# Attention and max-out FFN on one core: the second batch's softmax weights split undivided, its weighted sums divided, and an epsilon moved from VectorE to ScalarE

## The chip, the cores and the metric

The kernel runs on one core of a Trainium2 chip. The metric is the device time of one execution in microseconds (us); a comparison takes the median of several executions. A profile is one further execution, recorded with the start and the length of each instruction on TensorE (PE, its weight loads as PEld), VectorE (DVE), ScalarE (ACT), GpSimd (POOL) and the DMA queue that SyncE (SP) feeds.

## The reference

```python
# q, k, v: (8 batches, 12 heads, 448 rows, 64), float32
q_n, k_n = rmsnorm(q, g_q), rmsnorm(k, g_k)
scores = q_n @ k_n.T / sqrt(64)
attn = exp(scores - max(scores))              # "undivided" weights
attn = attn / (sum(attn) + 1e-9)              # "divided" weights
x = (attn @ v), heads side by side            # 3584 tokens x 768
h = maximum(maximum(x @ w1, x @ w2), x @ w3)  # three 768 x 768 layers
out = h @ w_out
```

## The kernel before

**Groups and quarters.** A group `g` is one batch's pair of heads, and there are 48: batch 0 is groups 0 to 5, the second batch 6 to 11, and so on. Each group is worked in four quarters `c` of 112 query rows. The quarter's scores for both heads (2 x 448 columns) lie in a PSUM tile `sc`, of which there are two in turn. So the scores of quarter c+2 can't start before the last reader of quarter c's tile is done.

**The first batch** (`g < PLAIN = 6`) multiplies in float32. Its exponentials go to SBUF and are turned by TensorE; the sums of a row's exponentials go to a tile `sum`. One group later the sums get their epsilon (`guard_sums`, ScalarE, L619), are inverted (`inverse_sums`, VectorE, L623), are spread over the 64 columns of a head by eight small float32 matmuls (`spread_sums`, L631), are copied to SBUF (`keep_sums`, ScalarE, L641), and multiply the weighted sums in PSUM (`scale_plain`, VectorE, L711).

**All later groups** split each operand into a float16 and a float16 rest, and add three products. A quarter runs like this:

- `scores` (L553, PE): six matmuls into `sc`.
- `row_max` (L562, DVE): the negated maximum of both heads' rows.
- `softmax` (L570 and L579, ACT): the scaled maximum `nm`, then one exponential for each head, written back into `sc`; the row sums go beside them in PSUM, each by a record named ACTIVATION_READ_ACCUMULATOR.
- `upper_weights`: the divisor `rs`, made by two VectorE instructions (L648: epsilon and scaling, L652: reciprocal); then ScalarE writes the divided float16 weights, one instruction for each head (L655).
- `lower_weights` (L665, DVE): the float16 rests, one instruction for each head. This one frees `sc`.
- `turn_weights`: a DMA transpose of both parts into `pt`. A group later `add_values` (L703, PE) multiplies with the values, and `finish` (L717 on ACT, L718 on DVE) splits the weighted sums into `xt`.

**The order** is written out by hand: `beat(g, i)` issues, for each of a group's twelve beats, attention work, and `thirds` fills in matmuls of the FFN of an earlier batch (L732 for the three layers, L796 for the last; their PSUM tiles `acc`, three buffers under the tag `m`, are read by `hidden`: L742 ACT, L746 DVE, L752 ACT, L756 DVE). Of a quarter, beat 3c issues the exponentials, beat 3c+1 `upper_weights`; what is due in between, such as the float16 copy of the next keys (`upper_rows`, L434) in each group's first quarter, stands between the two on ScalarE. Each engine works its own list in order. During the first two batches VectorE also decodes the float64 weights (L196, L200, L205 and others). The values of group g+6 are loaded in group g (`load_v`, `vr`, eight buffers), on SyncE's list, where key, query and weight loads and the transposes follow.

## Time and profile before

| what | before |
|---|---|
| time, median of 3 | 1100.64 us (1097.57 to 1104.33) |
| the profiled execution's own time | 1099.43 us |
| its span, first to last instruction | 1097.6 us |
| mean granted TensorE clock | 0.964 |
| PE busy | 1011.4 us (92%) |
| ACT busy | 771.8 us (70%) |
| DVE busy | 755.7 us (69%) |
| POOL busy | 704.2 us (64%) |

A group row of the page has: line, engine, operation, tile written<-tiles read, number of instructions; then the time in which at least one of them ran and the mean length of one in ns; then the idle time of the engine just before them, and what ended most of it. In a timeline row the first two numbers are start and length in us, and a bracket holds the idle time before. A row of waits has the total in us, the number, and the longest. A row of stretches has the length, each engine's busy time (with its instructions), the granted TensorE clock, the DMA share and GB/s.

### The profile page before, as it was taken

What the parts mean: (1) busy time and instruction counts of PE and PEld (TensorE: products, weight loads), DVE (VectorE), ACT (ScalarE), POOL (GpSimd) and SP (SyncE); (2) the same over time, 40 slices, a digit from 0 to 9 for tenths busy, and PEclk for the clock granted to TensorE, in tenths of its full rate; (3) what the DMA queues carried; (4) which work ended last, traced back from release to release, by engine and by line L of the source; (5) the groups of instructions that cost most, each with busy time, mean ns of one, the idle gap of its engine ahead of it and who ended that gap; (6) DMA issues with size and microseconds to landing.
All of it is one profiled execution on the core that took longest, in us unless ns stands there. A gap on an engine that the chain in (4) does not pass through costs nothing. (4 is left out here: it accounts for less than half of the span.)

```text
span 1097.6 us, 18387 instructions
## 1 busy us (share of the span) xinstructions
PE 1011.4 (92%) x6168; PEld 499.4 (45%) x6168; DVE 755.7 (69%) x1390; ACT 771.8 (70%) x1767; POOL 704.2 (64%) x805
## 2 busy tenths in 40 slices
PE   4678769888899999999999999999999999999998
PEld 2333334334444454444544454444444554445554
DVE  4799988888767676777677767777676766761110
ACT  4598888767878687787877787777777787863101
POOL 5477988866767777677777776777777677610000
PEclk9697869999999999999999999999999999999999
DMA  5554566855887779778887798787877797553002
GB/s 152 164 168 149 131 183 135 192 116 121 164 156 143 145 153 179 152 148 144 168 156 147 138 168 172 148 145 155 174 145 140 140 178 142 108 100 73 1 1 57
DMA packets 426493, 152.28 MB, mean 139 GB/s; under 512 B 372896, under 2 KB 422048, under 8 KB 426400
## 3 DMA queue, kind: packets, MB, share of 16 engines
q1 hardware_dynamic: 425888, 150.95, 67.7%
q8 instruction: 48, 0.79, 0.3%
q14 instruction: 45, 0.37, 0.1%
q10 hardware_dynamic: 512, 0.18, 0.1%
HBM read 51.97 MB, written 11.01 MB: 57 GB/s over the span
## 5 line engine op out<-in xcount | busy, mean ns | idle before, releaser
L732 PE MATMUL acc<-xt,w_sb 128*128 128x448 f16 x2592 | 516.8, 355 | 0.0
L732 PEld LDWEIGHTS <-w_sb 128*128 128x128 f16 x2592 | 244.1, 98 | 259.3 <-issue 47.9
L579 ACT ACTIVATE sc<-sc,nm,down 112x448 f32<-112x448 f32 x336 | 234.2, 697 | 11.2
L562 DVE TENSOR_REDUCE sc<-sc 112x2 f32<-112x896 f32 x192 | 209.6, 1092 | 46.0 <-PE sc L553 44.7
L655 ACT ACTIVATE pp<-sc,rs 112x448 f16<-112x448 f32 x336 | 194.8, 632 | 46.6 <-ACT sc L579 40.9
L665 DVE SCALAR_TENSOR_TENSOR pp<-sc,rs,pp 112x448 f16<-112x448 f32 x336 | 212.9, 675 | 3.4 <-ACT pp L655 2.9
L387 POOL TENSOR_TENSOR ri<-ri,half_neg 128x7 f32<-128x7 f32 x96 | 154.2, 1606 | 8.0
L553 PE MATMUL sc<-kt,qt 64*112 64x448 f16 x1008 | 131.9, 367 | 28.8 <-DVE pp L665 25.0
L570 ACT ACTIVATE nm<-sc,down 112x2 f32<-112x2 f32 x192 | 50.7, 264 | 147.5 <-DVE sc L562 146.1
L796 PE MATMUL acc<-wo_sb,ht 128*128 128x384 f16 x864 | 151.0, 329 | 1.5 <-DVE ht L756 0.8
L761 POOL COPY hx<-ht 128x128 f16<-128x128 f16 x48 | 15.5, 323 | 197.1 <-DVE ht L756 191.1
L796 PEld LDWEIGHTS <-ht 128*128 128x128 f16 x864 | 81.6, 99 | 67.2 <-issue 13.5
L703 PE MATMUL av<-pt,vp 128*64 128x448 f16 x1008 | 108.3, 356 | 0.0
L553 PEld LDWEIGHTS <-qt 64*112 64x112 f16 x1008 | 54.8, 126 | 98.3 <-issue 57.8
L648 DVE TENSOR_SCALAR rs<-sc 112x2 f32<-112x2 f32 x168 | 26.6, 158 | 94.6 <-ACT sc L579 94.6
L440 POOL TENSOR_TENSOR kp<-kn,kp 128x512 f16<-128x512 f32 x42 | 50.0, 1191 | 58.9 <-ACT kp L434 58.9
L703 PEld LDWEIGHTS <-vp 128*64 128x64 f16 x1008 | 49.6, 108 | 55.7 <-issue 30.0
L718 DVE SCALAR_TENSOR_TENSOR xt<-av,xt 128x448 f16<-128x448 f32 x42 | 26.2, 625 | 70.8 <-ACT xt L717 70.8
L372 DVE TENSOR_REDUCE ss<-sq 128x7 f32<-128x448 f32 x96 | 60.9, 635 | 10.6 <-ACT sq L363 6.6
L531 POOL TENSOR_TENSOR vp<-vr,vp 128x448 f16<-128x448 f32 x42 | 43.8, 1044 | 30.3 <-ACT vp L525 30.2
L440 POOL TENSOR_TENSOR qp<-qn,qp 112x512 f16<-112x512 f32 x42 | 49.2, 1173 | 19.8 <-ACT qp L434 19.8
L517 POOL TENSOR_SCALAR vr<-vr,v_up 128x448 f32<-128x448 f32 x42 | 61.1, 1456 | 0.0
(112 smaller groups left out, 1200.4 us busy)
## 6 DMA issues: line engine op xcount, KB each, us to landing
raw<-in_moe_w_dram SPq DMA_DIRECT2D x18, 768.0 KB, 4.5
qr<-in_q_dram SPq DMA_DIRECT2D x48, 224.0 KB, 3.1
vr<-in_v_dram SPq DMA_DIRECT2D x96, 96.0 KB, 2.6
kr<-in_k_dram SPq DMA_DIRECT2D x95, 96.0 KB, 3.1
raw<-in_moe_w_out_dram SPq DMA_DIRECT2D x6, 768.0 KB, 5.0
pt<-pp SPq DMA_TRANSPOSE x168, 4.0
out_dram<-osb SPq DMA_DIRECT2D x8, 336.0 KB, 3.2
out_dram<-osb SPq DMA_DIRECT2D x8, 288.0 KB, 3.6
```

The costliest lines, as they stand in the source:

```text
L372: nc.vector.tensor_reduce(sums[g % 2][:sq.shape[0], KQ[what]], sq, axis=AX, op=ALU.add)
L387: nc.gpsimd.tensor_tensor(out=ri, in0=ri, in1=half_neg[:, at], op=ALU.pow)
L440: nc.gpsimd.tensor_tensor(out=parts[:, 1], in0=n, in1=parts[:, 0], op=ALU.subtract)
L517: nc.gpsimd.tensor_scalar(out=vr, in0=vr, scalar1=v_up[:, g // NP:g // NP + 1], scalar2=None, op0=ALU.mult,)
L553: nc.tensor.matmul(sc[:QP, h, :S], qt[rows, qp, c], kt[rows, kp, KEYS[h]], start=n == 0, stop=n == len(TERMS) - 1,)
L562: nc.vector.tensor_reduce(sc[:QP, 0, S + 8:S + 10], sc[:QP, :, :S], axis=AX, op=ALU.max, negate=True)
L579: nc.scalar.activation(to, sc[:QP, h, :S], AF.Exp, bias=nm[:, h:h + 1], scale=down[:QP], accum_out=total,)
L655: nc.scalar.activation(pp[:, 0, h], sc[:QP, h, :S], AF.Copy, scale=rs[:, h:h + 1])
L665: nc.vector.scalar_tensor_tensor(out=pp[:, 1, h], in0=sc[:QP, h, :S], scalar=rs[:, h:h + 1], in1=pp[:, 0, h], op0=ALU.mult, op1=ALU.subtract,)
L703: nc.tensor.matmul(av[half, :S], vp[rows, group, vpart], pt[rows, 7 * wp + group], start=u == 0 and n == 0, stop=u == 3 and n == len(TERMS ...
L732: nc.tensor.matmul(acc[:, :S], wt[:, wp, c], xs[c][:, xp], start=(c == 0 and n == 0), stop=(c == NCT - 1 and n == 2),)
L796: nc.tensor.matmul(acc[:, :HW], lhs, wo_sb[:, f, wp, half * HW:(half + 1) * HW], start=(f == 0 and n == 0), stop=(f == NFT - 1 and n == 2),)
```

## The change

Three things change; a new constant `UNDIVIDED = 12` marks the end of the second batch.

1. Groups 6 to 11 write their weights undivided. The row sums go to `sum`, there is no `rs`, one ScalarE instruction writes `P_UP` times the exponentials of both heads, and one VectorE instruction writes both rests. The weighted sums are divided one group later as in the first batch (`guard_sums` to `scale_plain`). The tile `by` of `keep_sums` gets a buffer of its own in place of one shared with the FFN's `m`, and `vr` has seven buffers in place of eight.
2. Groups 12 to 47 still divide their weights. The epsilon and scaling of `rs` go from VectorE to ScalarE; the reciprocal stays on VectorE.
3. Nothing else in the order of `beat` changes.

```diff
+UNDIVIDED = 12
...
-        load_kv(g, "vr", v, 8)
+        load_kv(g, "vr", v, 7)
...  softmax
+        if g < UNDIVIDED and c == 0:
+            s["sum"] = sb.tile([QP, NQ, 2], F32, name="sum", bufs=2)
         if g < PLAIN:
-            if c == 0:
-                s["sum"] = sb.tile([QP, NQ, 2], F32, name="sum", bufs=2)
             s["e", c] = sb.tile([QP, 2, S], F32, name="e", tag="pp", bufs=3)
         for h in range(2):
             to, total = sc[:QP, h, :S], sc[:QP, 1, S + 8 + h:S + 9 + h]
+            if g < UNDIVIDED:
+                total = s["sum"][:, c, h:h + 1]
             if g < PLAIN:
-                to, total = s["e", c][:, h], s["sum"][:, c, h:h + 1]
+                to = s["e", c][:, h]
...  keep_sums
-        s["by"] = sb.tile([P, S], F32, name="by", tag="m", bufs=2)
+        s["by"] = sb.tile([P, S], F32, name="by", bufs=1)
...  upper_weights
+        if g < UNDIVIDED:
+            pp = s["pp", c] = sb.tile([QP, 2, 2, S], F16, name="pp", bufs=3)
+            nc.scalar.activation(pp[:, 0], sc[:QP, :, :S], AF.Copy, scale=P_UP)
+            return
         rs = sb.tile([QP, 2], F32, name="rs", bufs=3)
-        nc.vector.tensor_scalar(
-            out=rs, in0=sc[:QP, 1, S + 8:S + 10], scalar1=SUM_EPS, scalar2=1.0 / P_UP,
-            op0=ALU.add, op1=ALU.mult,
+        nc.scalar.activation(
+            rs, sc[:QP, 1, S + 8:S + 10], AF.Copy, bias=SUM_EPS / P_UP, scale=1.0 / P_UP
         )
         nc.vector.reciprocal(rs, rs)
...  lower_weights
+        if g < UNDIVIDED:
+            nc.vector.scalar_tensor_tensor(
+                out=pp[:, 1], in0=sc[:QP, :, :S], scalar=P_UP, in1=pp[:, 0],
+                op0=ALU.mult, op1=ALU.subtract,
+            )
+            return
...  beat
-        if 0 <= w < PLAIN:
+        if 0 <= w < UNDIVIDED:
```

VectorE's list in the second batch, from the maximum of group 7's first quarter to the rests of its first quarter. Before (`wo_sb` and `raw` are the decoding of the output weights, `ss` the sums of squares for a later group, `m` and `acc` the FFN):

```order
L562 TENSOR_REDUCE sc<-sc 112x2
L665 SCALAR_TENSOR_TENSOR pp<-sc,rs,pp 112x448 x2
L259 TENSOR_SCALAR w_most<-most 128x1
L262 RECIPROCAL w_up<-w_most 128x1
L263 TENSOR_SCALAR w_up<-w_up 128x1
L200 SCALAR_TENSOR_TENSOR wo_sb<-raw,wo_sb 128x768
L648 TENSOR_SCALAR rs<-sc 112x2
L652 RECIPROCAL rs<-rs 112x2
L205 SCALAR_TENSOR_TENSOR wo_sb<-raw,wo_sb 128x768
L372 TENSOR_REDUCE ss_87<-sq 128x7
```

The same place in the changed kernel, whose lines stand 3 to 15 lower:

```order
L565 TENSOR_REDUCE sc<-sc 112x2
L673 SCALAR_TENSOR_TENSOR pp<-sc,pp 112x896
L262 TENSOR_SCALAR w_most<-most 128x1
L265 RECIPROCAL w_up<-w_most 128x1
L266 TENSOR_SCALAR w_up<-w_up 128x1
L203 SCALAR_TENSOR_TENSOR wo_sb<-raw,wo_sb 128x768
L208 SCALAR_TENSOR_TENSOR wo_sb<-raw,wo_sb 128x768
L628 RECIPROCAL sum<-sum 112x8
L375 TENSOR_REDUCE ss_87<-sq 128x7
```

The two instructions on `rs` are gone, and with them VectorE's need of the exponentials at this place; the reciprocal of the group before's eight sums has come in.

ScalarE's list in the same quarter. Before:

```order
L570 ACTIVATE nm<-sc,down 112x2
L579 ACTIVATE sc<-sc,nm,down 112x448 x2
L434 CAST kp<-kn_90 128x512
L655 ACTIVATE pp<-sc,rs 112x448 x2
L434 CAST qp<-qn 112x512
```

In the changed kernel:

```order
L573 ACTIVATE nm<-sc,down 112x2
L584 ACTIVATE sc,sum<-sc,nm,down 112x448 x2
L437 CAST kp<-kn_90 128x512
L654 ACTIVATE pp<-sc 112x896
L624 ACTIVATE sum<-sum 112x8
L437 CAST qp<-qn 112x512
```

The weights' instruction is one, it no longer reads `rs`, and the epsilon for the group before's sums follows it.

ScalarE's list in a later batch, group 21, first and second quarter. Before:

```order
L570 ACTIVATE nm<-sc,down 112x2
L579 ACTIVATE sc<-sc,nm,down 112x448 x2
L434 CAST kp<-kn_90 128x512
L655 ACTIVATE pp<-sc,rs 112x448 x2
L434 CAST qp<-qn 112x512
L570 ACTIVATE nm<-sc,down 112x2
L579 ACTIVATE sc<-sc,nm,down 112x448 x2
L655 ACTIVATE pp<-sc,rs 112x448 x2
```

In the changed kernel:

```order
L573 ACTIVATE nm<-sc,down 112x2
L584 ACTIVATE sc<-sc,nm,down 112x448 x2
L437 CAST kp<-kn_90 128x512
L657 ACTIVATE rs<-sc 112x2
L663 ACTIVATE pp<-sc,rs 112x448 x2
L437 CAST qp<-qn 112x512
L573 ACTIVATE nm<-sc,down 112x2
L584 ACTIVATE sc<-sc,nm,down 112x448 x2
L657 ACTIVATE rs<-sc 112x2
L663 ACTIVATE pp<-sc,rs 112x448 x2
```

In the first quarter the new instruction stands behind the copy of the keys (`kp`), in the second right behind the exponentials.

On TensorE the only difference is six times eight matmuls of `spread_sums`, one set in the second quarter of each of groups 7 to 12, right behind the third quarter's scores. The lists of SyncE and GpSimd are the same.

More of the change, by code (lines that the diff above doesn't have):

```diff
@@ L662, in lower_weights @@
         s = st[g]
-        sc, rs, pp = s.pop(("sc", c)), s.pop(("rs", c)), s["pp", c]
+        sc, pp = s.pop(("sc", c)), s["pp", c]
+        if g < UNDIVIDED:
[4 more added lines that the diff above has]
+            return
+        rs = s.pop(("rs", c))
         for h in range(2):
```

## The prediction

> **What bounds the kernel now.** First the page: the span, and the groups of one quarter.

> ```profile
> span 1097.6 us, 18387 instructions
> L562 DVE TENSOR_REDUCE sc<-sc 112x2 f32<-112x896 f32 x192 | 209.6, 1092 | 46.0 <-PE sc L553 44.7
> L655 ACT ACTIVATE pp<-sc,rs 112x448 f16<-112x448 f32 x336 | 194.8, 632 | 46.6 <-ACT sc L579 40.9
> L553 PE MATMUL sc<-kt,qt 64*112 64x448 f16 x1008 | 131.9, 367 | 28.8 <-DVE pp L665 25.0
> L570 ACT ACTIVATE nm<-sc,down 112x2 f32<-112x2 f32 x192 | 50.7, 264 | 147.5 <-DVE sc L562 146.1
> L648 DVE TENSOR_SCALAR rs<-sc 112x2 f32<-112x2 f32 x168 | 26.6, 158 | 94.6 <-ACT sc L579 94.6
> ```

> TensorE's list has a fixed order, so the time is its work plus its gaps. Of the gaps behind the first batch nearly all stand before a quarter's scores (L553), which wait for VectorE's rests (L665) of two quarters earlier. VectorE itself idles 94.6 us at the divisor (L648), for the exponentials. Next the stretches: group 6, groups 7 to 11, groups 12 and 13, and the later groups to the last scores; then TensorE's waits from 160 to 330 us and behind that.

> ```profile
> 136.50:168.30 31.80, 21.08 (x98) 10.86 (x97) 27.14 (x46) 26.45 (x56) 28.54 (x26) 0.68 0.65 166
> 168.30:284.50 116.20, 100.67 (x616) 48.20 (x615) 98.76 (x175) 89.27 (x193) 88.38 (x91) 0.99 0.70 144
> 284.50:322.90 38.40, 34.40 (x213) 16.42 (x212) 26.11 (x53) 28.66 (x69) 28.29 (x33) 0.91 0.89 167
> 322.90:986.30 663.40, 657.13 (x4163) 319.68 (x4162) 474.29 (x932) 506.54 (x1187) 461.82 (x553) 1.00 0.79 150
> ...
> PE sc L553 <- DVE pp L665: 17.6, 10, 3.9
> ...
> PE sc L553 <- DVE pp L665: 5.7, 13, 1.3
> ```

> In the second batch TensorE idles 10.7 + 15.5 = 26.2 of 148.0 us (31.80 less 21.08, and 116.20 less 100.67). Later it idles 6.3 of 663.4 us: there only a delay that reaches the scores counts. I therefore reckon two terms, and each against the profiled execution (1099.43 us, 1.2 below the median shown).

> **Term A, the second batch.** Group 7, second quarter:

> ```profile
> 178.48 1.26 DVE L665 SCALAR_TENSOR_TENSOR pp<-sc,rs,pp 112x448 f16<-112x448 f32 x2
> 179.79 0.78 PE L553 MATMUL sc<-kt,qt 64*112 64x448 f16 x6 [1.96 <-DVE pp L665]
> 180.48 0.16 DVE L648 TENSOR_SCALAR rs<-sc 112x2 f32<-112x2 f32 x1 [0.73 <-ACT sc L579]
> 180.67 0.17 DVE L652 RECIPROCAL rs<-rs 112x2 f32<-112x2 f32 x1
> 180.75 0.67 DVE L372 TENSOR_REDUCE ss<-sq 112x8 f32<-112x512 f32 x1
> 180.92 1.16 ACT L655 ACTIVATE pp<-sc,rs 112x448 f16<-112x448 f32 x2 [0.48 <-ACT sc L579]
> ```

> VectorE loses the divisor, 0.27 us (180.48 to 180.75), and here the wait of 0.73 before it. The rests as one instruction are not in the trace: no shorter than one pass over 896 columns (L562, 1.09), no longer than the pair (1.26); I take 1.14, near L562, which has the same columns: 0.12 less. So 0.39 a quarter, 7.8 in groups 7 to 11. The weights as one ScalarE instruction lie between one of the pair (0.63) and the pair (1.16); I take 1.05, and ScalarE has 27 us to spare there. It no longer waits 0.48 for the divisor. The sums go to SBUF, as in the first batch. What each group adds is in the first batch's rows, by their shapes:

> ```profile
> L711 DVE TENSOR_TENSOR av<-av,by 128x448 f32<-128x448 f32 x6 | 3.7, 618 | 0.7 <-ACT by L641 0.7
> L641 ACT COPY by<-spread 128x448 f32<-128x448 f32 x6 | 3.2, 529 | 0.0
> L631 PE MATMUL spread<-ident,sum 112*64 112x112 f32 x96 | 5.9, 265 | 0.6 <-ACT pt L611 0.6
> L619 ACT ACTIVATE sum<-sum 112x8 f32<-112x8 f32 x6 | 1.4, 235 | 0.0
> L623 DVE RECIPROCAL sum<-sum 112x8 f32<-112x8 f32 x6 | 1.1, 188 | 0.0
> ```

> VectorE gets 0.62 + 0.19, 4.0 in five groups: its 98.8 us become 95.0, and most of its waits go. ScalarE gets 0.53 + 0.24 and gives back about 0.4. TensorE gets 5.9/6 = 0.99, 5.0 in five groups: its 100.7 become 105.6, now the longest of the three. It still waits where decoding stands in a lump between two maxima. I followed the rows of VectorE, ScalarE and TensorE from score to score through the five groups with these lengths and found 4.4 us of waits left (0.6, 0.1, 0.9, 1.5 and 1.3; 13.5 now). So 110.0 for 116.2: 6.2 less. Group 6, where VectorE's lead is what counts, gives 1.5, and group 12, whose quarters get the same division beside a ScalarE divisor, takes back 0.5: **A = -7.2**. Its bounds: +5.9 (all six sets in full, no wait shorter) and -20.3 (all 26.2 us of idling gone).

> Half clock follows the longest of these waits:

> ```profile
> 267.22 0.78 PE L553 MATMUL sc<-kt,qt 64*112 64x448 f16 x6 [3.22 <-DVE pp L665]
> 268.60:272.00 3.40, 3.40 (x12) 1.63 (x11) 2.78 (x5) 2.19 (x4) 2.16 (x3) 0.50 0.94 178
> 372.23 0.78 PE L553 MATMUL sc<-kt,qt 64*112 64x448 f16 x6 [1.25 <-DVE pp L665]
> ```

> After 3.22 us of waiting the clock is 0.50 for 3.4 us, which costs 1.7; after 1.25 us (372.23) the later stretch stays at 1.00. My bookkeeping leaves 1.3 us at 267: **-1.5** for the clock, between 0 and -1.7. [...]

> **Term B, the later batches.** Group 21, from the end of the first quarter's sums to the third quarter's scores:

> ```profile
> 466.17 0.13 ACT L579 ACTIVATION_READ_ACCUMULATOR sc<-sc,nm,down 112x1 f32 x1
> 466.23 0.62 ACT L434 CAST kp<-kn 128x512 f16<-128x512 f32 x1
> 466.34 0.16 DVE L648 TENSOR_SCALAR rs<-sc 112x2 f32<-112x2 f32 x1 [0.74 <-ACT sc L579]
> 466.54 0.17 DVE L652 RECIPROCAL rs<-rs 112x2 f32<-112x2 f32 x1
> 466.79 1.16 ACT L655 ACTIVATE pp<-sc,rs 112x448 f16<-112x448 f32 x2
> 467.66 1.09 DVE L562 TENSOR_REDUCE sc<-sc 112x2 f32<-112x896 f32 x1
> 468.66 1.27 DVE L665 SCALAR_TENSOR_TENSOR pp<-sc,rs,pp 112x448 f16<-112x448 f32 x2
> 469.98 0.78 PE L553 MATMUL sc<-kt,qt 64*112 64x448 f16 x6
> ```

> Now the divisor is ready at 466.71, since VectorE takes the sums the moment they are there (466.30), while ScalarE copies the keys. The ScalarE divisor isn't in the trace. Its bounds: L648, 0.16, which reads the same two columns, and L641's 0.53 for 448 columns; I take 0.26 from L570, the same engine on two PSUM columns. It starts behind the key copy, at about 466.78, and ends at 467.04; the reciprocal ends at 467.25, **0.5 us later**. Queued behind that reciprocal on VectorE are the next maximum (467.66) and the rests (468.66), and the third quarter's scores started 0.05 us behind those. So this group pays nearly all of it. In the other quarters, with nothing in between, the same count gives +0.10 where VectorE waits for the sums, and -0.12 in fourth quarters where it comes late. An FFN copy that also stands there makes the first quarter's delay 0.8 (`m`) or 1.0 (`osb`); where it is `ht`, VectorE waits for that copy anyway, and the delay is 0.25.

> What a group pays is its delay, with what is left from the group before, less the room before the third scores. The pattern repeats every 12 groups: the wait of 1.25 us at 372.23 comes again at 608.12, 235.9 later.

> ```profile
> 608.12 0.77 PE L553 MATMUL sc<-kt,qt 64*112 64x448 f16 x6 [1.26 <-DVE pp L665]
> ...
> 409.10 1.28 DVE L665 SCALAR_TENSOR_TENSOR pp<-sc,rs,pp 112x448 f16<-112x448 f32 x2
> 411.38 0.77 PE L553 MATMUL sc<-kt,qt 64*112 64x448 f16 x6
> ```

> Of 12 groups, six have no room (as 21) and pay 0.65, 0.36, 0.65, 0.13, 0.38 and 0.13; four have 0.3 to 1.0 (group 18, above: 410.38 to 411.38) and pay 0.30, 0.26, 0.29 and 0.47; two have over 1.0 and pay next to nothing. That is 3.7 for 12 groups, and for groups 12 to 47, the last of which have room, **B = +10**. Its bounds: 0 (room takes all) and +22 (each of 36 groups pays 0.6). [...]

> **Term D, the seventh buffer.** Group 7's values now wait for the first group's weighted sums:

> ```profile
> vr<-in_v_dram SPq DMA_DIRECT2D x96, 96.0 KB, 2.6
> ...
> 47.09 3.38 PE L692 MATMUL av<-pt,vr 128*64 128x448 f32 x16
> 56.04 0.61 DVE L170 TENSOR_REDUCE v_rows<-vr 128x1 f32<-128x448 f32 x1
> ```

> Those end at 50.5. At the page's 2.6 us to land, the load's four pieces, issued one after the other, are there before VectorE reads them at 56.04; at twice that, as beside a weight load, they would be late by about 1. The loads of groups 8 to 10 wait in the same way, with more time. I take **+0.5**, between 0 and 1.5. Queued behind on SyncE stand a weight load and the next keys, needed much later.

> The sum is -7.2 - 1.5 + 10 + 0.5 = **+1.8**: 1101.2 for such an execution, 1102 beside the median.

> **The rivals.** (1) *Slower: the divisor behind ScalarE's queue.* If lateness adds up from group to group instead of being taken up by the room, each of 36 groups pays 0.6, B is +22, the sum -7.2 - 1.5 + 22 + 0.5 = +13.8, and the time 1114. It decides from a delay above 0.4 to 1.0 us, the room in half of the groups. For it: six groups without room. Against: VectorE idles one to two us at most fourth maxima. [...] (2) *Faster: the waits go and the room holds.* If four fifths of the 26.2 us go (21.0, less 5.9 for the sets) and B is 1, the change is -15.1 - 1.5 + 1 + 0.5 = -15.1, and the time 1085.5. For it: VectorE stops waiting for exponentials. Against: the decoding stays, and it stands in lumps. (3) *The division doesn't relieve:* the spread sums hold one of three `m` buffers until ScalarE copies them, and the FFN's matmuls wait for it, 1 to 2 us in each of six groups: 6 to 12 on top of my sum, 1108 to 1114. For it: no wait in the trace shows how near that is. Against: the next `acc` is begun only when a whole unit of 18 matmuls is done.

> **How the numbers follow.** My forecast 0.66, the rivals 0.15, 0.13 and 0.06. A and B are each uncertain by some 5 us, so the forecast's own range is 1094 to 1110. The full range goes on towards rivals 1 and 2 until one in ten is left out at each end: 1089 to 1113. A measurement of this kernel can tell about 1% (11 us) from no change. Faster by more than that is rival 2 less its nearer part: 0.11. Slower by more: most of rival 1, half of rival 3 and 3 in 100 of the forecast: 0.18. Within: 0.71.

> **What would show it.** A: waits of L553 from 136 to 285 us near 8 instead of 19 to 21 us, this stretch near 140 us; spread rows of 0.99 each; the clock at 1.00 near 260. B: idle time before L553 in the later groups up from about 6 to 16 us, at third quarters, and reciprocals that wait for ScalarE. D: v_rows near 56 without a wait over 1.5. I am wrong if ScalarE's divisor costs nothing at the scores, or if the second batch gives under 3 or over 12.

## The result and the profile after

The changed kernel takes 1115.08 us (median of 6 runs, 1112.61 to 1117.42) against 1098.34 us for the kernel before in the same comparison: a ratio of 1.0143, 95% interval 1.0123 to 1.0164, so about 16 us slower. The prediction was 1102 us with a range of 1089 to 1113. The profiled execution took 1115.59 us; its page gives the span and the scores like this (lines stand 3 to 15 lower; scores are L556):

```profile
span 1113.8 us, 18664 instructions
L556 PE MATMUL sc<-kt,qt 64*112 64x448 f16 x1008 | 133.1, 370 | 30.6 <-DVE pp L673 16.2
```

The 28.8 us that TensorE idled before scores became 30.6, and rests of the second batch (L673) still end most of it. The stretches that the prediction showed, from score to score in the changed kernel: group 6, groups 7 to 11, groups 12 and 13, and the later groups.

```profile
135.20:164.40 29.20, 20.59 (x100) 11.13 (x99) 26.02 (x33) 24.46 (x50) 26.65 (x25) 0.67 0.68 177
164.40:295.80 131.40, 114.79 (x698) 56.29 (x697) 93.16 (x126) 89.01 (x185) 89.13 (x93) 0.90 0.62 129
295.80:334.90 39.10, 34.54 (x231) 17.01 (x230) 25.15 (x46) 30.43 (x79) 26.95 (x31) 0.96 0.91 163
334.90:1002.00 667.10, 656.78 (x4159) 318.68 (x4160) 448.77 (x797) 526.20 (x1322) 461.56 (x553) 1.00 0.78 148
```

Group 6 became 2.6 us shorter and the 34 later groups 3.7 us longer. The loss is in groups 7 to 11: 131.4 us for 116.2, where 110.0 were predicted. TensorE is busy there for 114.79 us instead of 100.67, and its granted clock is 0.90 instead of 0.99. VectorE's work fell further than planned, from 98.8 to 93.2 us (95.0 were planned), and TensorE's idle time did not fall: 16.6 us (131.40 less 114.79) against 15.5. Its waits for the rests became 12.1 us where they had been 12.7, and 4.5 us of waits before the added sets came in.

**One group shows how.** Group 8 in the changed kernel, from the keys' copy in its first quarter to the added set in its second; rows of VectorE, ScalarE and TensorE:

```profile
195.44 0.60 ACT L437 CAST kp<-kn 128x512 f16<-128x512 f32 x1
195.95 0.92 ACT L654 ACTIVATE pp<-sc 112x896 f16<-112x896 f32 x1
196.76 0.20 ACT L624 ACTIVATE sum<-sum 112x8 f32<-112x8 f32 x1
196.99 0.20 DVE L628 RECIPROCAL sum<-sum 112x8 f32<-112x8 f32 x1 [2.46 <-ACT sum L624]
...
198.13 1.09 DVE L565 TENSOR_REDUCE sc<-sc 112x2 f32<-112x896 f32 x1
...
199.12 1.08 DVE L673 SCALAR_TENSOR_TENSOR pp<-sc,pp 112x896 f16<-112x896 f32 x1
...
200.26 0.78 PE L556 MATMUL sc<-kt,qt 64*112 64x448 f16 x6 [1.38 <-DVE pp L673]
...
201.67 0.62 DVE L771 SCALAR_TENSOR_TENSOR ht<-acc,ht 128x448 f16<-128x448 f32 x1 [1.00 <-ACT ht L767]
...
202.35 1.76 PE L636 MATMUL spread<-ident,sum 112*64 112x112 f32 x16 [1.32 <-DVE ht L771]
```

Read it from the top. VectorE stands 2.46 us before the reciprocal of the group before's sums (L628), because ScalarE makes their epsilon (L624) only behind the keys' copy and the merged weights. Behind L628 on VectorE stand the next maximum (L565) and the rests (L673) that free the scores' tile; TensorE waits 1.38 us for them. Then the set (L636) is at the head of TensorE's list, and TensorE waits again, 1.32 us, for an `m` buffer which VectorE's hidden rows (L771) free. The set itself takes 1.76 us where the first batch's took 0.99: the granted clock is 0.50 here. Half clock stands near the third quarter's scores in all five groups (the same columns as above; the clock is the number ahead of the last two):

```profile
178.20:181.60 3.40, 3.40 (x13) 1.34 (x10) 1.52 (x2) 3.33 (x9) 2.74 (x3) 0.50 0.76 162
202.10:205.50 3.40, 3.15 (x20) 2.00 (x21) 3.40 (x5) 0.77 (x2) 3.06 (x3) 0.50 0.64 138
226.00:232.80 6.80, 6.26 (x31) 3.23 (x32) 5.37 (x7) 6.18 (x13) 6.48 (x10) 0.50 0.78 157
253.30:260.10 6.80, 5.21 (x26) 2.90 (x27) 3.37 (x8) 4.80 (x10) 2.96 (x6) 0.50 0.68 133
280.60:287.40 6.80, 5.79 (x31) 3.23 (x32) 3.44 (x5) 3.02 (x8) 4.25 (x7) 0.50 0.68 138
```

That is 27.2 us at half clock; the kernel before had one such stretch there, of 3.4 us. In four of the five groups the half clock begins before the set does (in group 8 at 202.10 and 202.35, in group 9 at 226.0 and 227.84): there it follows the waits, and the set runs in it. The sets of groups 7 to 11 by themselves, with their second wait, which stands in three of the five groups:

```profile
L636 PE MATMUL spread<-ident,sum 112*64 112x112 f32 x80 | 8.1, 375 | 4.5 <-DVE o_up L295 2.4 <-DVE ht L771 2.0
```

So of the 15.2 us that this stretch became longer, 8.1 are the sets' own time, at half clock for the most part, some 6.0 the other matmuls at half clock (an estimate: 114.79 - 100.67 - 8.1), and 1.1 more idle time. The size of the half clock is that of one execution: kernel 2 below has the same lists in these groups, and its profiled execution shows 13.6 us of half clock and a stretch of 125.9 us, with a granted clock of 0.95 in it.

### The profile page after: what moved, and what is told of

Same layout as the page of the kernel before. It is cut to its first block, busy times and chain, and to the rows that moved or that the text cites. A ratio compares the mean times of both kernels' runs of the same rounds, so it can differ in the third digit from the quotient of the medians.

```text
span 1113.8 us, 18664 instructions
## 1 busy us (share of the span) xinstructions
PE 1021.8 (92%) x6264; PEld 506.0 (45%) x6264; DVE 721.2 (65%) x1186; ACT 792.1 (71%) x1899; POOL 702.2 (63%) x805
## 4 chain that ended last, share of the span: by engine, by line
PE 54%; DVE 21%; ACT 16%; issue 6%; DMA 1%; SPq 1%; POOL 0%; DVEq 0%; ACTq 0%; POOLq 0%
PE acc L747 24%; PE acc L811 11%; PE av L718 9%; PE sc L556 7%; DVE sc L565 6%; ACT sc L584 4%; DVE pp L680 4%; ACT pp L663 2%; ACT e L584 2%; ACT xt L732 1%; DVE most L173 1%; ACT nm L573 1%; DVE m L761 1%; DVE ss L375 1%; DVE v_rows L173 1%
## 5 line engine op out<-in xcount | busy, mean ns | idle before, releaser
L565 DVE TENSOR_REDUCE sc<-sc 112x2 f32<-112x896 f32 x192 | 209.5, 1091 | 48.4 <-PE sc L556 47.1
L663 ACT ACTIVATE pp<-sc,rs 112x448 f16<-112x448 f32 x288 | 166.8, 630 | 35.0 <-DVE rs L660 33.9
L680 DVE SCALAR_TENSOR_TENSOR pp<-sc,rs,pp 112x448 f16<-112x448 f32 x288 | 182.4, 675 | 0.2 <-ACT pp L663 0.2
L556 PE MATMUL sc<-kt,qt 64*112 64x448 f16 x1008 | 133.1, 370 | 30.6 <-DVE pp L673 16.2
L573 ACT ACTIVATE nm<-sc,down 112x2 f32<-112x2 f32 x192 | 50.5, 263 | 151.1 <-DVE sc L565 151.0
L776 POOL COPY hx<-ht 128x128 f16<-128x128 f16 x48 | 15.5, 323 | 202.8 <-DVE ht L771 195.5
L660 DVE RECIPROCAL rs<-rs 112x2 f32<-112x2 f32 x144 | 23.7, 165 | 143.4 <-ACT rs L657 143.4
L556 PEld LDWEIGHTS <-qt 64*112 64x112 f16 x1008 | 54.0, 127 | 101.8 <-issue 55.4
L443 POOL TENSOR_TENSOR kp<-kn,kp 128x512 f16<-128x512 f32 x42 | 50.7, 1207 | 58.9 <-ACT rs L657 37.4
L733 DVE SCALAR_TENSOR_TENSOR xt<-av,xt 128x448 f16<-128x448 f32 x42 | 26.2, 624 | 69.2 <-ACT xt L732 69.2
```

The costliest lines, as they stand in the source:

```text
L443: nc.gpsimd.tensor_tensor(out=parts[:, 1], in0=n, in1=parts[:, 0], op=ALU.subtract)
L556: nc.tensor.matmul(sc[:QP, h, :S], qt[rows, qp, c], kt[rows, kp, KEYS[h]], start=n == 0, stop=n == len(TERMS) - 1,)
L565: nc.vector.tensor_reduce(sc[:QP, 0, S + 8:S + 10], sc[:QP, :, :S], axis=AX, op=ALU.max, negate=True)
L573: nc.scalar.activation(nm, sc[:QP, 0, S + 8:S + 10], AF.Copy, scale=down[:QP])
L663: nc.scalar.activation(pp[:, 0, h], sc[:QP, h, :S], AF.Copy, scale=rs[:, h:h + 1])
L680: nc.vector.scalar_tensor_tensor(out=pp[:, 1, h], in0=sc[:QP, h, :S], scalar=rs[:, h:h + 1], in1=pp[:, 0, h], op0=ALU.mult, op1=ALU.subtract,)
```

## The experiments

The theories, by the names that the expectations use. **H1**: the added sets are the loss, with the half clock that follows them. **H2**: ScalarE's divisor (part 2) is the loss. **H3**: the sets cost their own time and their wait for an `m` buffer, and no more. **H4**: the merged instructions or the new buffers. **H5**: VectorE's relief is spent in new waits for ScalarE; **H6**: such waits would only move on. Ratios are to the kernel before, with 95% intervals; "7 to 11" is the stretch of those five groups in the profiled execution.

| kernel | median us | ratio | 7 to 11 |
|---|---|---|---|
| before | 1098.3 to 1099.3 | 1 | 116.2 |
| the change | 1115.1 | 1.0143 (1.0123 to 1.0164) | 131.4 |
| 1 ScalarE's divisor alone | 1109.4 | 1.0098 (1.0083 to 1.0112) | 122.2 |
| 2 second batch alone | 1109.7 | 1.0098 (1.0082 to 1.0114) | 125.9 |
| 3 change without the sets | 1102.0 | 1.0030 (1.0019 to 1.0042) | 117.1 |
| 4 before with the sets | 1108.3 | 1.0087 (1.0065 to 1.0108) | 123.7 |
| 5 as 3, reciprocal later | 1100.5 | 1.0017 (1.0005 to 1.0028) | 113.8 |
| 6 change, sets behind the FFN | 1104.9 | 1.0054 (1.0038 to 1.0070) | 122.3 |
| 7 as 2, with both moves | 1099.1 | 1.0001 (0.9991 to 1.0010) | 118.2 |
| 8 as 7, wide sets | 1103.1 | 1.0041 (1.0027 to 1.0055) | 121.5 |
| 9 as 7, sets in beat 7 | 1096.3 | 0.9962 (0.9943 to 0.9981) | 112.6 |
| 10 as 7, VectorE's hidden rows | 1098.7 | 0.9993 (0.9979 to 1.0007) | 118.8 |
| 11 both of 9 and 10 | 1095.8 | 0.9959 (0.9940 to 0.9978) | 115.9 |
| 12 before, VectorE's hidden rows | 1100.6 | 1.0004 (0.9992 to 1.0016) | 117.7 |

**1. ScalarE's divisor alone.** The kernel before, with this edit:

```diff
-        nc.vector.tensor_scalar(
-            out=rs, in0=sc[:QP, 1, S + 8:S + 10], scalar1=SUM_EPS, scalar2=1.0 / P_UP,
-            op0=ALU.add, op1=ALU.mult,
-        )
+        nc.scalar.activation(
+            rs, sc[:QP, 1, S + 8:S + 10], AF.Copy, bias=SUM_EPS / P_UP, scale=1.0 / P_UP
+        )
```

> The kernel before with one edit of the change alone: ScalarE forms the divisor of every divided quarter (groups 6 to 47). Theory H1 (the loss is the spread sets on TensorE in the second batch and the half clock that follows them; the divisor on ScalarE costs the later batches about 4 us): 1100 to 1104 us against 1098.3 before, no half clock in groups 7 to 11. Rival H2 (the divisor behind ScalarE's queue is the loss, in the second batch too): 1110 to 1115 us, half the scores of groups 7 to 11 later by 2 us and more.

Measured 1109.4 us, 10.8 more than before: both expectations missed. H2's missed narrowly, and H1's because it forgot that here groups 6 to 11 get the divisor too, which in the change have none; nor is the clock full there, with 0.94 in the stretch and 13.6 us at half clock. The view of waits (total, number, longest), groups 7 to 11:

```profile
DVE rs L651 <- ACT rs L648: 20.9, 18, 3.0
```

VectorE waits 20.9 us there for the divisor, where before it waited 8.1 us for the exponentials. So behind a loaded ScalarE queue the divisor does cost something, with the half clock 6.0 us in five groups (122.2 less 116.2); but the change doesn't put it there.

**2. The second batch alone.** The change with the divisor of groups 12 to 47 left on VectorE (the edit above undone).

> The changed kernel with the divisor of groups 12 to 47 given back to VectorE: what is left is the second batch's edits. H1: 1109 to 1113 us, with the five half-clock stretches in groups 7 to 11. H2: 1098 us or less. If the parts add, this run's loss and that of the divisor alone make the change's 16.7 us together.

1109.7 us, of which groups 7 to 11 lose 9.7 (125.9 less 116.2): H1's number, with four half-clock stretches of 3.4 us and not the five of the change, and H2 falls for the change. Against the change the ratio is 0.0045 lower: the divisor in the later 36 groups costs 4.9 us (0.0045 x 1098.6; by the intervals 2 to 8, and by the later stretches of the two traces 3.8, 667.1 less 663.3). The losses of kernels 1 and 2, 10.8 each, do not add up to the change's, since both touch the second batch.

**3. The change without the sets.** For groups 6 to 11:

```diff
     def spread_sums(g):
+        if g >= PLAIN:
+            return
...  keep_sums
+        if g >= PLAIN:
+            nc.scalar.activation(
+                s["by"].rearrange("p (o d) -> p o d", o=4),
+                ident[:, 0:QP].rearrange("p (o d) -> p o d", o=1).broadcast_to([P, 4, QP]),
+                AF.Copy, scale=1.0 / 512,
+            )
+            return
```

> The changed kernel without the six added spread sets (it leaves out the spreading of the second batch's sums: the scale tile is filled by ScalarE from a constant, in the place where ScalarE copied the set). H1: 1096 to 1101 us, no half clock in groups 7 to 11, TensorE busy there near 100 us again instead of 114.8. Rival H4 (merged instructions, the own scale tile or the seventh buffer make the loss): 1110 us or more.

```profile
164.70:281.80 117.10, 102.16 (x618) 48.35 (x617) 93.42 (x126) 89.42 (x185) 87.98 (x92) 0.97 0.71 145
```

This kernel leaves out the spreading of the second batch's sums, so it serves for its time alone. 1102.0 us: by the ratios the sets cost 12.4 us of the change's 16 (0.0143 less 0.0030), not 5.9. But H1 isn't all: it had 1096 to 1101 and no half clock, where two stretches of 3.4 us are left, and with the relief that the prediction counted this stretch should have become 11 us shorter than before. It is 0.9 us longer. VectorE works 5.3 us less and TensorE waits as much as ever. The waits of this stretch, first before:

```profile
PE sc L553 <- DVE pp L665: 12.7, 8, 3.2
DVE rs L648 <- ACT sc L579: 8.1, 12, 1.2
DVE sc L562 <- PE sc L553: 1.7, 2, 1.2
DVE ht L756 <- ACT ht L752: 0.6, 1, 0.6
```

and in this kernel:

```profile
PE sc L556 <- DVE pp L682: 14.7, 8, 3.6
DVE ht L780 <- ACT ht L776: 7.4, 5, 2.4
DVE sum L628 <- ACT sum L624: 6.0, 2, 3.5
DVE sc L565 <- PE sc L556: 4.7, 3, 2.5
```

The 8.1 us at the divisor are gone, and 13.4 us stand at two other instructions that need ScalarE (7.4 + 6.0; 0.6 before). That gave H5. H4 falls: what is left of this kernel's loss is no more than the later groups' divisor (kernel 2), so merged instructions and buffers lose nothing that these runs can tell.

**4. The sets on the kernel before.** Weights and divisions as before; seven value buffers.

```diff
+    some = const.tile([QP, NQ, 2], F32, name="some")
+    nc.vector.memset(some, 1.0)
...  spread_sums
-        rs = s.pop("sum").rearrange("p c (h o) -> p c h o", o=1)
+        rs = (s.pop("sum") if g < PLAIN else some).rearrange("p c (h o) -> p c h o", o=1)
...  keep_sums
+        if g >= PLAIN:
+            unused = sb.tile([P, S], F32, name="unused", bufs=1)
+            nc.scalar.copy(unused, s.pop("spread")[:, :S])
+            return
...  beat
+        if PLAIN <= w < UNDIVIDED:
+            if i == 5:
+                spread_sums(w)
+            if i == 6:
+                keep_sums(w)
```

> The kernel before with six more spread sets in groups 6 to 11 at the place where the change has them, made from a constant and copied by ScalarE into a tile that nobody reads (value buffers seven as in the change, for the room); divisions and weights as before. H1: the sets alone bring the half clock: 1108 to 1113 us, five stretches of half clock in groups 7 to 11. Rival H3 (the sets cost their own time and the wait for their m buffer, no more): 1103 to 1107 us, full clock. Rival H4: 1098 to 1100 us.

1108.3 us by the median, in H1's bounds; the profiled execution, at 1105.7 us the quickest of four, is in H3's, with two half-clock stretches and not five (the clock is 0.97 in groups 7 to 11). So the sets alone, at this place, cost 9.6 us (0.0087 x 1098.6), most of the loss, whatever the weights do; how much half clock they bring differs from execution to execution. In this trace one set waits 3.67 us for its `m` buffer, which VectorE frees with `o_up`, a step of the decoding of the output weights:

```profile
253.31 1.19 PE L635 MATMUL spread<-ident,some 112*64 112x112 f32 x16 [3.67 <-DVE o_up L296]
```

**5. The reciprocal later.** Kernel 3 (without the sets) with

```diff
-            if i == 2:
+            if i == (2 if w < PLAIN else 4):
                 inverse_sums(w)
```

> The kernel without the added sets of the earlier run (the spreading of the second batch's sums is left out), with VectorE's reciprocal of the second batch's sums issued two beats later (beat 4 in place of 2), behind the row maximum and the weights that scores wait for. Theory H5 (VectorE's relief is spent in a new wait: its queue stands 6.0 us in groups 7 to 11 before this reciprocal, for ScalarE's epsilon): that wait goes to under 1 us and the scores' 14.7 us of waits to 9 to 11, so 1097 to 1100 us against 1102.0 with the reciprocal in its place. Rival H6 (VectorE would only wait elsewhere, for ScalarE's hidden rows or for scores): waits of the scores 13 us and more, 1101 to 1103 us.

```profile
PE sc L556 <- DVE pp L682: 11.0, 7, 3.9
DVE ht L780 <- ACT ht L776: 7.4, 5, 2.3
```

The wait at L628 is gone and TensorE's waits for the rests fall from 14.7 to 11.0 us; the stretch falls from 117.1 to 113.8. By the medians (1100.5 and 1102.0, with intervals that overlap) it can't be told from nothing; the sign is H5's, and the size 1.5 us, a quarter of VectorE's wait.

**6. The sets behind the FFN's matmuls.** The change with

```diff
-            if i == 5:
+            if i == 5 and w < PLAIN:
                 spread_sums(w)
...
         thirds(THIRDS[i] + (len(queue) > 1 and i % 6 == 4))
+        if i == 5 and PLAIN <= w < UNDIVIDED:
+            spread_sums(w)
```

> The changed kernel with the six added sets issued behind the FFN's matmuls of beat 5 instead of right behind the scores; all else as in the change. H1 with the place as the cause (a set right behind the scores' wait leaves a window of 3.4 us with little else in it, and the half clock follows): half clock in groups 7 to 11 from 27 us to 14 us or less, 1105 to 1110 us. H1 with the set itself as the cause (its small matmuls bring the half clock wherever they stand, or it still waits for its m buffer): 1112 to 1116 us.

```profile
164.70:287.00 122.30, 108.78 (x695) 52.62 (x694) 93.04 (x127) 90.23 (x187) 90.55 (x94) 0.96 0.71 139
```

The same sets a few matmuls later: 1104.9 us, 10 less than the change and just under the first expectation, the clock 0.96, and in group 8 (TensorE's rows) the set at its 0.99:

```profile
201.79 0.78 PE L556 MATMUL sc<-kt,qt 64*112 64x448 f16 x6 [1.38 <-DVE pp L673]
202.50 1.31 PE L747 MATMUL acc<-xt,w_sb 128*128 128x448 f16 x6
203.88 0.99 PE L636 MATMUL spread<-ident,sum 112*64 112x112 f32 x16
```

The wait before the scores is the 1.38 us of the change. What is gone here is the second wait, for the buffer, right behind the first; in the five groups it fell from 4.5 to 1.2 us, and the half clock from 27.2 to 10.2 us in these two executions. So it is the place that makes the sets cost more than their own time; how much of that is the wait and how much the half clock was not separated.

**7. Both moves, and the divisor on VectorE.** Kernel 2 with the edits of 5 and 6.

> The second batch's edits alone (divisor of the later groups on VectorE), with the sets behind the FFN's matmuls and the reciprocal of the sums two beats later. If H1 with the place and H5 both hold: 1099 to 1104 us against 1109.7 for the second batch's edits alone. If neither: 1108 to 1111 us.

1099.1 us: the second batch's edits, which cost 11 us as they stand, cost nothing when set and reciprocal are moved. It is at the quick end of what H1 with the place and H5 gave.

**8. Wide sets.** Kernel 7, where GpSimd first copies the eight inverse sums to 64 columns each (`wide`), and a set is

```diff
+            for c in range(NQ):
+                nc.tensor.matmul(
+                    spread[:, c * QP:(c + 1) * QP],
+                    wide[:QP, c * P:(c + 1) * P], ident[:QP, :QP],
+                    start=True, stop=True,
+                )
```

> As the combined run, but each added set as four matmuls of 128 columns instead of eight of 64: GpSimd copies the inverse sums out to both heads' columns first. If a set's own time counts (0.99 us at full clock), it falls to about 0.5: 2 to 4 us below the combined run, with half clock no more than there. If the number of matmuls doesn't matter, or GpSimd's copy comes late and the set waits for it: the combined run's time or above.

1103.1 us, 4 more than kernel 7; the stretch is 3.3 longer. Its waits show the sets' weight load waiting for a GpSimd instruction:

```profile
PEld spread L643 <- POOL ri L386: 2.5, 2, 2.3
```

Here fewer matmuls, with a GpSimd copy ahead of them, did not help; whether the copy alone explains the 4 us was not settled.

**9. The sets two beats later.** Kernel 7 with

```diff
-            if i == 6:
+            if i == (6 if w < PLAIN else 8):
                 keep_sums(w)
...
-        if i == 5 and PLAIN <= w < UNDIVIDED:
+        if i == 7 and PLAIN <= w < UNDIVIDED:
             spread_sums(w)
```

> The combined run with the sets two beats later (behind the FFN's matmuls of beat 7, copied out in beat 8). If the 2.7 us that TensorE still stands before the sets in groups 7 to 11 (for an m buffer) belong to beat 5, 1 to 3 us below the combined run (1096 to 1098 us); if the sets wait for an m buffer wherever they stand, the combined run's 1099 us.

```profile
168.60:281.20 112.60, 104.81 (x698) 52.19 (x697) 91.71 (x125) 87.83 (x183) 87.80 (x92) 0.98 0.76 149
```

1096.3 us, 0.9962 (0.9943 to 0.9981): faster than both kernels. TensorE's row in group 8 shows why; the set stands between weighted sums and scores and waits for nothing:

```profile
202.84 2.58 PE L719 MATMUL av<-pt,vp 128*64 128x448 f16 x24
205.35 0.99 PE L636 MATMUL spread<-ident,sum 112*64 112x112 f32 x16
206.55 0.77 PE L556 MATMUL sc<-kt,qt 64*112 64x448 f16 x6 [0.21 <-DVE pp L674]
```

TensorE's idle time in the stretch is 7.8 us (112.60 less 104.81) where before had 15.5: here is relief of the kind that the prediction counted on, 7.7 us, of which the sets take back 5 x 0.99.

**10 to 12. VectorE makes the first block's hidden rows.** Kernels 7, 9 and the one before, with

```diff
-                nc.scalar.activation(ht[:, 0], most, AF.Copy, scale=H_DOWN)
+                if b == 0:
+                    nc.vector.tensor_scalar(
+                        out=ht[:, 0], in0=most, scalar1=H_DOWN, scalar2=None, op0=ALU.mult
+                    )
+                else:
+                    nc.scalar.activation(ht[:, 0], most, AF.Copy, scale=H_DOWN)
```

> The combined run with the upper parts of the first block's hidden rows made by VectorE, not ScalarE. VectorE stood 7.6 us in groups 7 to 11 before the lower parts, for ScalarE's upper ones. H5 (VectorE's relief goes into waits for ScalarE): these waits go, scores' waits from 8.6 to 5 to 7 us, 1095 to 1098 us. Rival (VectorE's wait there is not on the way to the scores, and its added work, 6 x 0.5 to 0.7 us, is): 1099 to 1102 us.

> Both edits, sets two beats later and VectorE's hidden rows: 1093 to 1097 us if both theories hold, and then faster than the kernel before (1098.9) by 2 to 5 us.

> The kernel before with VectorE's hidden rows alone, to see how much of the last two runs has nothing to do with the undivided weights. In the kernel before VectorE stood only 1.0 us before these rows in groups 7 to 11, and is the engine that scores wait for: 1099 to 1103 us. If it is 1097 us or less, what the last two gain is this edit's and not the relief's.

1098.7, 1095.8 and 1100.6 us: next to kernels 7, 9 and before, none differs by more than its interval. The first lies between its two expectations, the other two lie in theirs. In the first of them VectorE's 7.6 us of waits for ScalarE's hidden rows are gone, and these stand in their place:

```profile
DVE sc L565 <- PE sc L556: 13.5, 5, 5.4
PE sc L556 <- DVE pp L674: 9.4, 7, 2.7
```

In kernel 7 the two were 9.7 and 8.6. So taking this wait away brought the scores nothing: H6 holds for the hidden rows, and for the reciprocal H5 holds at most in part (kernel 5). What kernel 11 gains is kernel 9's gain.

## Why the prediction was wrong, point by point

By the ratios the change's 0.0143 divide into the sets with 0.0113 (change less kernel 3: 12.4 us), the later groups' divisor with 0.0045 (change less kernel 2: 4.9 us), and the rest, relief and buffers, with -0.0015 (-1.6 us). By the intervals each of these is good to about 3 us, so the rest can't be told from nothing. The prediction had +5.9, +10 and -14.1.

- **Term A, the sets: the step that failed first.** "TensorE gets 5.9/6 = 0.99" priced a set as matmul time. At its place a set also waits for an `m` buffer (4.5 us in five groups), behind a wait for the rests that was there already; the clock was 0.50 for 27.2 us of the profiled execution, and four of the five sets took 1.76 us each, not 0.99. Kernels 3, 4 and 6 show it. The prediction's third rival had the buffer, but the wrong way round (the FFN waiting for the set), at 6 in 100, and said that no wait in the trace showed how near that was. One did: in the kernel before, groups 7 to 11, `marks`, a small matmul of the decoding that takes a buffer of the same three, waits for VectorE's hidden rows. The prediction's sum of 105.6 and 4.4 us has no place for these two us.

```profile
PE marks L155 <- DVE ht L756: 1.9, 1, 1.9
```

- **Term A, the relief: the step that failed second.** "4.4 us of waits left" of 13.5 came from following the rows by hand with the reciprocal as 0.19 us of work. It has ScalarE's epsilon ahead of it, and that stands behind key copy and merged weights. VectorE waits there 4.9 us, in two of the groups (6.0 without the sets), with the maximum and the rests queued behind it; and where VectorE comes early at the hidden rows, it waits 8.3 us for ScalarE (rows below, groups 7 to 11 of the change). VectorE lost its waits for the exponentials, and met ScalarE again. Kernel 3 shows no relief at all; 5 shows perhaps 1.5 us of it by its time, and 9 half of TensorE's idle time gone. That the reciprocal's wait alone kept the relief away is not shown: why the rest of the counted relief failed stays open, since taking away the wait at the hidden rows (kernel 10) brought nothing.

```profile
DVE ht L771 <- ACT ht L767: 8.3, 5, 2.4
DVE sum L628 <- ACT sum L624: 4.9, 2, 2.5
```

- **The clock: wrong in sign.** -1.5 was counted for one stretch of half clock less; in the profiled execution there were five, 27.2 us in all. Nor was TensorE idle throughout the 3.41 us ahead of the loss near 267 us in the kernel before: the wait of 3.22 us began earlier, and TensorE was busy for 1.36 of those 3.41 us (last section).
- **The merged instructions:** right, and kinder than taken: rests 1.14 taken, 1.08 measured; weights 1.05 taken, 0.91 measured.

```profile
L673 DVE SCALAR_TENSOR_TENSOR pp<-sc,pp 112x896 f16<-112x896 f32 x20 | 21.6, 1078 | 0.0
L654 ACT ACTIVATE pp<-sc 112x896 f16<-112x896 f32 x21 | 19.2, 914 | 0.1
```

- **Term B: mechanism right, size half.** The divisor was mis-sized (the row of the later stretch, and group 21's first quarter):

```profile
L657 ACT ACTIVATE rs<-sc 112x2 f32<-112x2 f32 x135 | 24.0, 177 | 2.2
...
478.73 0.13 ACT L584 ACTIVATION_READ_ACCUMULATOR sc<-sc,nm,down 112x1 f32 x1
478.78 0.62 ACT L437 CAST kp<-kn 128x512 f16<-128x512 f32 x1
479.29 0.18 ACT L657 ACTIVATE rs<-sc 112x2 f32<-112x2 f32 x1
479.50 0.17 DVE L660 RECIPROCAL rs<-rs 112x2 f32<-112x2 f32 x1 [1.34 <-ACT rs L657]
```

  0.18 us, not 0.26; the reciprocal ends 0.81 us behind the sums where it ended 0.41 behind them, so 0.40 later and not 0.5. TensorE's idle time in the later stretch rose by 4.0 us (10.3 against 6.3), not 10. With 0.1 less for each of the ten groups that pay, the prediction's 3.7 us for 12 groups become 2.7, and B about 7 (an estimate: 10 x 2.7/3.7); what made it less still was not followed.
- **Term D, the seventh buffer,** had +0.5 for a late load, and the load was not late: VectorE reads group 7's values at 55.29 us and those of groups 8 to 10 after them, none with a wait. Kernel 9 has seven buffers and is faster than before.
- **The rivals.** The time of the first, 1114, was nearly met, by another mechanism: its delays behind ScalarE's queue cost 4.9 us where it had 22. The prediction's own test ("spread rows of 0.99 each; the clock at 1.00 near 260") named the two lines that turned out wrong.

## What to carry to other kernels

Before work is put at a place in an in-order list, ask what it needs there and what stands right ahead of it: the same six sets of small matmuls cost 12 us right behind a wait, and moved behind other matmuls two beats later, with the reciprocal moved too and the later divisor left on VectorE, the kernel is 0.4% faster than before. Taking work off the engine that is waited for can bring nothing when that engine meets the same partner again at a later instruction: look through its queue for the next operand from there. Whether moving that instruction helps has to be tried, for of the two waits followed here one gave some 1.5 us that can't be told from nothing, and the other nothing.

## What the runs showed of the hardware

```profile
174.77:178.17 3.40, 1.51 (x22) 1.12 (x21) 3.40 (x5) 2.42 (x6) 3.32 (x4) 1.00 1.09 241
249.85:253.26 3.41, 1.71 (x12) 0.70 (x9) 3.41 (x5) 2.46 (x6) 3.24 (x6) 1.00 0.89 175
```

In the kernel before, a window with 1.46 us was followed by full clock, and the one with 1.36 us ahead of the stretch that the prediction shows (268.60) by half clock:

```profile
176.42:179.83 3.41, 1.46 (x10) 0.68 (x9) 3.32 (x5) 2.19 (x6) 3.41 (x4) 1.00 1.01 255
265.17:268.58 3.41, 1.36 (x10) 0.76 (x10) 3.34 (x8) 3.27 (x8) 0.80 (x2) 1.00 0.23 75
```

Of the changed kernel's windows at half clock, those from 178.20 and 202.10 (above), busy for 3.40 and 3.15 us, were followed by full clock; those from 226.00, 253.30 and 280.60, busy for 2.86, 1.81 and 2.39 us, were followed by half clock again. Spread sets took 0.20 and 1.76 us of the first two, and 1.56, 1.76 and 1.02 us of the other three. How much a set counts, and what exactly decides between the windows of 1.4 to 1.7 us, the runs do not show.
